# One-hot matrices from 16-bit operands, token column innermost, in a Trainium2 attention-and-experts kernel

## The chip, the cores and the metric

The kernel runs on one core of one Trainium2 chip. The metric is the device time of one execution in microseconds. The profile names the engines: PE is TensorE (matrix products; PEld is its weight load), DVE is VectorE, ACT is ScalarE, POOL is GpSimd and SP is SyncE, which only issues transfers.

## The reference

Three steps follow each other. Lines are left out at "...".

```python
def _attn_ref(q, k, v, g_norm):            # 8 batches, 8 heads, 576 tokens, 64 wide
    kv = np.einsum('bhsd,bhse->bhde', k, v)
    out = np.einsum('bhsd,bhde->bhse', q, kv)
    ...                                    # divided by its rms, times g_norm
def _moe_ref(x, w_gate, w1, w2):           # x: 4608 tokens x 512; 8 experts
    cap = N // E                           # 576 tokens for each expert
    logits = x @ w_gate
    order = np.argsort(-logits.flatten())
    for idx in order:                      # greedy, best score first
        tok, e = (int(idx) // E, int(idx) % E)
        if assigned[tok] >= 0 or counts[e] >= cap:
            continue
        assigned[tok] = e
        counts[e] += 1
    ...
        h = np.maximum(x[mask] @ w1[e], 0.0)
        out[mask] = h @ w2[e]
def _moe2_ref(x, w_in, w_out):             # 512 -> 2048 -> 512
    h = x @ w_in
    return (h * np.cos(h)) @ w_out
```

What matters here is the assignment: it gives each expert a list of exactly 576 tokens, and the kernel needs that list as row numbers, because it gathers those rows of x and later scatters the results with indirect transfers.

## The kernel before, in words

**Stages.** The first 148 us or so hold the attention, which writes the normalised rows of x to a table in device memory (`x_rows`). Then a router of eight *phases* (`Router.phase`, k = 0 to 7) finds, phase by phase, the expert that fills up next and its 576 tokens. Phase 0 runs before the experts' work, phases 1 to 7 are spread between the expert products of the experts before. The rest is 16 units of 288 tokens (two for each expert): products with w1 (`h`), with w2 (`y`), with w_in and the cosine (`h2`), and with w_out (`outs`), all in three-term 16-bit products.

**A phase.** It picks each token's best open expert (`m`, `oh`, `mx`, `ohb`), searches the 576th best score in eight rounds of comparing and counting (`cmp`, `cn`, `g`, `nS`), takes the winning expert (`wi` are the rows of its weights, which POOL then loads), and numbers the chosen tokens: `po` is each token's place in the list, or 0 for a token not chosen. The token numbers are laid out as 128 partitions x 36 columns (`NCOL`).

**The list.** The place p = 32 c + r of each token is taken apart into r = p & 31 (`qi`) and c = p >> 5 (`ci`). For 12 columns at a time (a *group*, three groups in a phase) VectorE forms `A`, 128 x 12 x 32, which is 1 where r equals the position in the last dimension; `Bm` (named `B` in the profile), 128 x 12 x 20, the same for c; and `Bi` (named `Bm` in the profile), 128 x 12 x 2 x 20, which is that times the two halves of the token's number (`C.ids`: number >> 6 and number & 63). TensorE then adds up 36 products `A[column] x Bi[column]`, 32 x 40 each, in one PSUM tile `p`. `low`, `new`, `idx` and `edge` read it and put the row numbers together, and POOL gathers the rows of x by `idx`.

**What sets the order.** The program is recorded by a planner (`Sched`, `Meter`): each instruction is charged a time by its shape, not by its type (`us = 0.07 + 0.06 * scalars + n / 960` for most VectorE operations), and the router's steps are slipped between the expert products where these planned clocks leave room. Each engine then runs its list strictly in that order. A step more, or a longer one, so moves other steps. The tile `pq` in PSUM has one buffer, and the transposes of x and the small products of the weights' scales (`psb`) share it.

**Lines.** `Router.phase` stands at line 274, the place's parts at 423, the groups at 430 to 445, `make_consts` with the counter `i32` and `ids` at 474 to 505. All instructions carry the line of one recording helper (687), so rows are told apart by the names of tiles.

Of the kernel before, what the change touches and what calls it, by code (L numbers as in the profile page):

```python
# [8 lines left out]
F32 = mybir.dt.float32  # L9
F16 = mybir.dt.float16  # L10
BF = mybir.dt.bfloat16
I32 = mybir.dt.int32
AF = mybir.ActivationFunctionType
OP = mybir.AluOpType
# [7 lines left out]
NCOL = 36  # L22
# [236 lines left out]
class Router:  # L259
# [14 lines left out]
    def phase(self, k):  # L274
        nc, wk, C, L = self.nc, self.wk, self.C, self.L
        V = nc.vector
# [6 lines left out]
        else:  # L283
# [23 lines left out]
            base = wk.tile([128, 1], F32, name="base")  # L307
            yield "result"
            nS = None
            for half in range(2):  # L310
                for r in range(4):
# [16 lines left out]
                    p = self.pt()  # L328
# [3 lines left out]
                    else:  # L332
                        for g in range(9):
                            c = slice(4 * g, 4 * g + 4)
# [5 lines left out]
                        p = self.pt()  # L340
# [3 lines left out]
                    g = wk.tile([16, E], BF, name="g1")  # L344
                    V.tensor_scalar(g[0:n], p[0:n, 0:E], CAP - 0.5, step, op0=OP.is_ge, op1=OP.mult)
                    yield "result"
                    p = self.pt()
# [13 lines left out]
            w = wk.tile([128, E], F32, name="w")  # L361
# [25 lines left out]
        if last:  # L387
            eh = None
            w = wk.tile([128, E], F32, name="w")
# [18 lines left out]
        if not last:  # L408
# [9 lines left out]
                               op0=OP.add, op1=OP.mult)  # L418
        po = wk.tile([128, NCOL], F32, name="po")
        V.tensor_add(po, pv[:, 0], pv[:, 1])  # L420
        pi = wk.tile([128, NCOL], I32, name="pi")
        V.tensor_scalar(pi, po, -1.0, None, op0=OP.add)
        qi = wk.tile([128, NCOL], I32, name="qi")
        V.tensor_scalar(qi, pi, 31, None, op0=OP.bitwise_and)
        ci = wk.tile([128, NCOL], I32, name="ci")
        V.tensor_scalar(ci, pi, 5, None, op0=OP.arith_shift_right)
        yield "vector"
        p = self.pt()
        G = 12
        for g in range(NCOL // G):  # L430
            c = slice(g * G, g * G + G)
            A = wk.tile([128, G, 32], BF, name="A", bufs=2)
            V.tensor_tensor(A, qi[:, c, None].to_broadcast([128, G, 32]),
                            C.i32[:, None, :].to_broadcast([128, G, 32]), op=OP.is_equal)
            yield "vector"
            Bm = wk.tile([128, G, 20], BF, name="B1")
            V.tensor_tensor(Bm, ci[:, c, None].to_broadcast([128, G, 20]),
                            C.i32[:, None, 0:20].to_broadcast([128, G, 20]), op=OP.is_equal)
            Bi = wk.tile([128, G, 2, 20], BF, name="Bm", bufs=2)
            V.tensor_tensor(Bi, Bm[:, :, None, :].to_broadcast([128, G, 2, 20]),  # L440
                            C.ids[:, c, :, None].to_broadcast([128, G, 2, 20]), op=OP.mult)
            yield "result"
            for i in range(G):
                nc.tensor.matmul(p[0:32, 0:40], A[:, i, :], Bi[:, i].rearrange("p h s -> p (h s)"), start=(g + i == 0),
                                 stop=(g * G + i == NCOL - 1))
        V.tensor_sub(self.un, self.un, v[:, 0])
        V.tensor_sub(self.un, self.un, v[:, 1])
# [26 lines left out]
def make_consts(nc, sb, w, C):  # L474

    V, G = nc.vector, nc.gpsimd
    jp = w[:, 0:128]
    G.iota(jp, pattern=[[1, 128]], base=0, channel_multiplier=-1)
    C.ident = sb.tile([128, 128], F32, name="ident")
    V.tensor_scalar(C.ident, jp, 0.0, None, op0=OP.is_equal)  # L480
    C.tri = sb.tile([128, 128], BF, name="tri")
    V.tensor_scalar(C.tri, jp, 0.0, None, op0=OP.is_gt)
    C.ones = sb.tile([128, 128], BF, name="ones")
    V.memset(C.ones, 1.0)
    C.i32 = sb.tile([128, 32], F32, name="i32")
    G.iota(C.i32, pattern=[[1, 32]], base=0, channel_multiplier=0, allow_small_or_imprecise_dtypes=True)
    C.i16 = sb.tile([128, 4, 16], F32, name="i16")
    for r in range(4):
        s = 1 << (12 - 4 * r)
        G.iota(C.i16[:, r], pattern=[[s, 16]], base=0, channel_multiplier=0, allow_small_or_imprecise_dtypes=True)  # L490
    i32 = w[0:32, 128:160]
    G.iota(i32, pattern=[[-1, 32]], base=0, channel_multiplier=1)
    C.sel = sb.tile([32, 4, E], F16, name="sel")
    V.tensor_scalar(C.sel.rearrange("p c e -> p (c e)"), i32, 0.0, None, op0=OP.is_equal)
    C.w8 = sb.tile([128, E], F32, name="w8")
    G.iota(C.w8, pattern=[[-1, E]], base=E, channel_multiplier=0, allow_small_or_imprecise_dtypes=True)
    C.ip4 = sb.tile([128, 4], F32, name="ip4")
    G.iota(C.ip4, pattern=[[128, 4]], base=0, channel_multiplier=1, allow_small_or_imprecise_dtypes=True)
    ids = w[:, 160:160 + NCOL]
    G.iota(ids.rearrange("p (s r) -> p s r", r=RB), pattern=[[2 * S, B // 2], [1, RB]], base=0, channel_multiplier=RB)  # L500
    C.ids = sb.tile([128, NCOL, 2], F32, name="ids")
    V.tensor_scalar(w[:, 200:200 + NCOL], ids, 6, None, op0=OP.arith_shift_right)
    V.tensor_copy(C.ids[:, :, 0], w[:, 200:200 + NCOL])
    V.tensor_scalar(w[:, 240:240 + NCOL], ids, 63, None, op0=OP.bitwise_and)
    V.tensor_copy(C.ids[:, :, 1], w[:, 240:240 + NCOL])

# [365 lines left out]
class Moe:  # L874
# [103 lines left out]
    def dense(self, sc):  # L978
# [35 lines left out]
        for i, (which, a, j) in enumerate(units):  # L1014
# [5 lines left out]
            if j == 0:  # L1020
                side = "A" if side == "B" else "B"
                if side in self.used:
# [413 lines left out]
def body(ctx, tc, q, k, v, g_norm, w_gate, w1, w2, w_in, w_out, out):  # L1436
# [4 lines left out]
    sm = ctx.enter_context(tc.tile_pool(name="sm", bufs=2))  # L1441
    C = Consts()
    make_consts(nc, pers, sm.tile([128, 512], I32, name="dG", bufs=DG), C)
    gcol = pers.tile([128, 1], F32, name="gcol")
    for s in range(2):
# [158 lines left out]
```

## Time and profile before

| | us |
|---|---|
| median of 3 runs | 1442.72 |
| lowest and highest | 1441.85, 1450.02 |
| the profiled execution, its own time | 1443.92 |
| span of its trace | 1442.2 |
| PE busy | 1330.7 (92%) |
| DVE busy | 901.0 (62%) |
| ACT busy | 615.4 (43%) |
| POOL busy | 165.3 (11%) |

Busy shares are means over the whole span; what an engine's work is worth is read in its stretch. A matmul's duration holds its way through the engine's pipeline, so that twelve of 0.18 us each may stand in 0.47 us. The chain of waits goes back from the last instruction, at each step to what released it.

### The profile page before, as it was taken

The page shows a single profiled execution, that of the slowest core. Times are in us where ns is not written, and L with a number is a line of the kernel's source. Part 1 is how long each engine was busy: PE and PEld are TensorE (multiplying, and loading weights), DVE is VectorE, ACT ScalarE, POOL GpSimd, SP SyncE. Part 2 cuts the span into 40 slices and gives each one's busy share as a digit, 9 for nine tenths or more (in the row PEclk, how much of TensorE's full clock was granted, in tenths as well). Part 3 has the DMA queues.
Part 4 walks back from the last instruction along what each step waited for, and adds up shares of the span by engine and source line. Part 5 has one row for each costly group of instructions (what it writes and reads, how often), then busy time and mean ns, then how long its engine had stood idle before and what let it go on. Part 6 is the DMA issues. An engine that isn't in the chain of part 4 may idle for free.

```text
span 1442.2 us, 28591 instructions
## 1 busy us (share of the span) xinstructions
PE 1330.7 (92%) x12072; PEld 906.4 (63%) x12072; DVE 901.0 (62%) x2136; ACT 615.4 (43%) x1031; POOL 165.3 (11%) x195
## 2 busy tenths in 40 slices
PE   5777258989999999999999999999999999999997
PEld 4665235746666674757575756767676667667663
DVE  2668888879578674786578656654466336544350
ACT  2567364737255430546054602553356125424140
POOL 0000130012012011040003100320021002000000
PEclk9889569999999999999999999999999999999999
DMA  8896452213023011041003200220022002000000
GB/s 295 306 353 245 156 161 92 74 67 104 8 67 93 16 59 45 1 127 44 8 8 101 66 9 16 95 75 1 15 93 74 8 16 74 16 1 15 8 8 22
DMA packets 40368, 109.63 MB, mean 76 GB/s; under 512 B 4272, under 2 KB 12464, under 8 KB 39728
## 3 DMA queue, kind: packets, MB, share of 16 engines
q0 software_dynamic: 15744, 62.70, 13.0%
q1 hardware_dynamic: 23808, 45.09, 9.0%
q8 instruction: 94, 1.54, 0.4%
q14 instruction: 34, 0.28, 0.1%
q10 hardware_dynamic: 688, 0.02, 0.0%
HBM read 88.78 MB, written 19.02 MB: 75 GB/s over the span
## 4 chain that ended last, share of the span: by engine, by line
PE 83%; DVE 9%; issue 3%; ACT 2%; DMA 2%; POOL 1%; ACTq 0%; POOLq 0%; DVEq 0%
PE ph L687 74%; PE pr L687 3%; PE pT L687 2%; PE P L687 1%; PE pO L687 1%; PE pq L687 1%; DVE stB L687 1%; DVE SS L687 1%; DMA wgr<-in_moe_w_gate_dram 1%; DVE stA L687 1%; DVE cmp L687 1%; DVE eg L687 1%; DVE qTs L687 1%; DVE w1s L687 1%; DVE wout L687 0%
## 5 line engine op out<-in xcount | busy, mean ns | idle before, releaser
L687 PE MATMUL ph<-wout,gT 128*128 128x512 f16 x1728 | 392.4, 381 | 7.3 <-ACT wout L687 3.9
L687 PE MATMUL ph<-yT,win 128*128 128x288 f16 x3072 | 384.1, 286 | 1.4 <-DVE eg L687 1.4
L687 PEld LDWEIGHTS <-win 128*128 128x128 f16 x3072 | 297.9, 98 | 81.3 <-DVE eg L687 2.4
L687 PEld LDWEIGHTS <-gT 128*128 128x128 f16 x1728 | 162.4, 98 | 193.7 <-issue 7.2
L687 ACT ACTIVATE ek<-ph,quarter,us 128x576 int32<-128x576 f32 x128 | 106.1, 829 | 324.3 <-PE ph L687 308.8
L687 PE MATMUL ph<-xT,w1s 128*128 128x288 f16 x1536 | 201.3, 290 | 7.5 <-DVE hT L687 6.5
L687 PE MATMUL ph<-hT,w2s 128*128 128x288 f16 x1536 | 201.7, 286 | 0.0
L687 DVE SCALAR_TENSOR_TENSOR et<-ph,us,ek 128x576 f32<-128x576 f32 x128 | 104.6, 817 | 132.4 <-ACT ek L687 129.6
L687 PEld LDWEIGHTS <-w1s 128*128 128x128 f16 x1536 | 148.8, 99 | 47.7 <-issue 4.9
L687 PEld LDWEIGHTS <-w2s 128*128 128x128 f16 x1536 | 146.4, 98 | 36.2
L687 POOL DMA_INDIRECT out_dram<-eg,idx x36 | 38.3, 1064 | 620.5 <-DVE scT L687 291.5
L687 DVE SCALAR_TENSOR_TENSOR eg<-ph,cG,et 128x576 f32<-128x576 f32 x128 | 103.6, 809 | 2.7 <-ACT et L687 1.3
L687 DVE TENSOR_TENSOR gT<-eg,gT 128x576 f16<-128x576 f32 (+2 forms) x192 | 99.6, 550 | 0.7
L687 ACT ACTIVATE et<-et,qtr 128x576 f32<-128x576 f32 x128 | 97.8, 764 | 0.0
L687 ACT ACTIVATE gT<-eg 128x576 f16<-128x576 f32 (+2 forms) x192 | 92.0, 511 | 12.0 <-DVE eg L687 12.0
L687 DVE TENSOR_TENSOR eg<-ph,scT 128x512 f32<-128x512 f32 x36 | 24.9, 692 | 104.5 <-PE ph L687 100.7
L687 ACT ACTIVATE yT<-ph,sy 128x576 f16<-128x576 f32 x32 | 21.9, 736 | 139.9 <-DVE sy L687 137.4
L687 DVE SCALAR_TENSOR_TENSOR hT<-ph,hT 128x576 f16<-128x576 f32 x64 | 48.2, 755 | 49.4 <-ACT hT L687 49.2
L687 ACT ACTIVATE hT<-ph 128x576 f16<-128x576 f32 x64 | 41.1, 645 | 88.7 <-PE ph L687 87.2
L687 POOL DMA_INDIRECT io<-x_rows,idx x35 | 39.7, 1135 | 254.4 <-PE pq L687 202.4
L687 POOL DMA_INDIRECT stA<-in_moe_w_dram,wi x28 | 35.5, 1270 | 199.8 <-issue 193.1
L687 PE MATMUL pO<-KV,qTs 64*64 64x72 f32 x1152 | 38.2, 248 | 13.2 <-issue 12.3
(213 smaller groups left out, 1299.2 us busy)
## 6 DMA issues: line engine op xcount, KB each, us to landing
kt<-in_k_dram SPq DMA_DIRECT2D x16, 576.0 KB, 6.2
vt<-in_v_dram SPq DMA_DIRECT2D x16, 576.0 KB, 7.6
qt<-in_q_dram SPq DMA_DIRECT2D x16, 576.0 KB, 7.8
io<-in_moe_w_in_dram SPq DMA_DIRECT2D x16, 512.0 KB, 6.9
io<-in_moe_w_out_dram SPq DMA_DIRECT2D x16, 512.0 KB, 3.6
x_rows<-xs POOLq DMA_DIRECT2D x3, 2340.0 KB
x_rows<-wout POOLq DMA_DIRECT2D x1, 2340.0 KB
out_dram<-eg,idx POOLq DMA_INDIRECT x36
```

The lines of the kernel that those rows point to most:

```text
L687: return f(*a, **kw)
```

## The change

The one-hot matrices are laid out with the 12 token columns as the last dimension and formed from bfloat16 operands alone. Both parts of the place go into one tile `qc`, which one more instruction (`CAST qb<-qc`, 128 x 72) turns to bfloat16. The counter is written out for all 12 columns (`i32g`, 128 x 32 x 12, one CAST at the program's start), and `ids` is kept as two rows of 36 in bfloat16. TensorE reads `A[:, :, i]` and `Bi[:, :, :, i]`: the elements of one product lie 12 elements (24 bytes) apart where they lay side by side. The numbers and shapes of the products, and of the three VectorE operations in a group, are as before.

```diff
@@ Router.phase
-        qi = wk.tile([128, NCOL], I32, name="qi")
-        V.tensor_scalar(qi, pi, 31, None, op0=OP.bitwise_and)
-        ci = wk.tile([128, NCOL], I32, name="ci")
-        V.tensor_scalar(ci, pi, 5, None, op0=OP.arith_shift_right)
+        qc = wk.tile([128, 2, NCOL], I32, name="qc")
+        V.tensor_scalar(qc[:, 0], pi, 31, None, op0=OP.bitwise_and)
+        V.tensor_scalar(qc[:, 1], pi, 5, None, op0=OP.arith_shift_right)
+        qb = wk.tile([128, 2, NCOL], BF, name="qb")
+        V.tensor_copy(qb, qc)
...
-            A = wk.tile([128, G, 32], BF, name="A", bufs=2)
-            V.tensor_tensor(A, qi[:, c, None].to_broadcast([128, G, 32]),
-                            C.i32[:, None, :].to_broadcast([128, G, 32]), op=OP.is_equal)
+            A = wk.tile([128, 32, G], BF, name="A", bufs=2)
+            V.tensor_tensor(A, qb[:, 0, None, c].to_broadcast([128, 32, G]), C.i32g, op=OP.is_equal)
...
-            Bm = wk.tile([128, G, 20], BF, name="B1")
-            V.tensor_tensor(Bm, ci[:, c, None].to_broadcast([128, G, 20]),
-                            C.i32[:, None, 0:20].to_broadcast([128, G, 20]), op=OP.is_equal)
-            Bi = wk.tile([128, G, 2, 20], BF, name="Bm", bufs=2)
-            V.tensor_tensor(Bi, Bm[:, :, None, :].to_broadcast([128, G, 2, 20]),
-                            C.ids[:, c, :, None].to_broadcast([128, G, 2, 20]), op=OP.mult)
+            Bm = wk.tile([128, 20, G], BF, name="B1")
+            V.tensor_tensor(Bm, qb[:, 1, None, c].to_broadcast([128, 20, G]), C.i32g[:, 0:20], op=OP.is_equal)
+            Bi = wk.tile([128, 2, 20, G], BF, name="Bm", bufs=2)
+            V.tensor_tensor(Bi, Bm[:, None].to_broadcast([128, 2, 20, G]),
+                            C.ids[:, :, None, c].to_broadcast([128, 2, 20, G]), op=OP.mult)
...
-                nc.tensor.matmul(p[0:32, 0:40], A[:, i, :], Bi[:, i].rearrange("p h s -> p (h s)"), start=(g + i == 0),
+                nc.tensor.matmul(p[0:32, 0:40], A[:, :, i], Bi[:, :, :, i].rearrange("p h s -> p (h s)"), start=(g + i == 0),
@@ make_consts
-    C.i32 = sb.tile([128, 32], F32, name="i32")
-    G.iota(C.i32, pattern=[[1, 32]], base=0, channel_multiplier=0, allow_small_or_imprecise_dtypes=True)
+    C.i32g = sb.tile([128, 32, 12], BF, name="i32g")
+    i32 = w[:, 280:312]
+    G.iota(i32, pattern=[[1, 32]], base=0, channel_multiplier=0)
+    V.tensor_copy(C.i32g, i32[:, :, None].to_broadcast([128, 32, 12]))
...
-    C.ids = sb.tile([128, NCOL, 2], F32, name="ids")
+    C.ids = sb.tile([128, 2, NCOL], BF, name="ids")
...
-    V.tensor_copy(C.ids[:, :, 0], w[:, 200:200 + NCOL])
+    V.tensor_copy(C.ids[:, 0], w[:, 200:200 + NCOL])
...
-    V.tensor_copy(C.ids[:, :, 1], w[:, 240:240 + NCOL])
+    V.tensor_copy(C.ids[:, 1], w[:, 240:240 + NCOL])
```

The planner charges the new CAST, and some steps move. Outside phase 0 and the stretch between phases 1 and 2 only a few rows do.

VectorE in phase 1, from the place to the next search; before (`psm`, `psb`: the weights' scale of the next expert; `low` to `idx`: the list; `m`: the next phase's start):

```order
L687 TENSOR_SCALAR qi<-pi 128x36
L687 TENSOR_SCALAR ci<-pi 128x36
...
L687 TENSOR_TENSOR un<-un,v 128x36 x2
L687 COPY low<-pr 32x20
L687 SCALAR_TENSOR_TENSOR new<-pr,low 32x1 x4
L687 TENSOR_TENSOR idx<-edge,new 128x1
L687 SCALAR_TENSOR_TENSOR idx<-pr,low 32x4 x4
L687 TENSOR_REDUCE psm<-am_4506 128x1
L687 TENSOR_SCALAR psb<-psm,g_95 128x1
L687 TENSOR_REDUCE m<-L 128x36
```

and after:

```order
L688 TENSOR_SCALAR qc<-pi 128x36 x2
L688 CAST qb<-qc 128x72
...
L688 TENSOR_TENSOR un<-un,v 128x36 x2
L688 TENSOR_REDUCE psm<-am_4509 128x1
L688 TENSOR_SCALAR psb<-psm,g_96 128x1
L688 TENSOR_SCALAR peb<-pq 128x1
L688 TENSOR_SCALAR s_4535<-peb 128x1
L688 TENSOR_TENSOR sg<-s_4535,gcol 128x1
L688 COPY low<-pr 32x20
L688 SCALAR_TENSOR_TENSOR new<-pr,low 32x1 x4
L688 TENSOR_TENSOR idx<-edge,new 128x1
```

The scale of the next expert's w1 now stands ahead of the list. On TensorE its product `pq<-psb,ones` follows 3 products with w_out behind phase 1's last group where it followed 12, and 18 instead of 15 products with w_out stand ahead of the first group.

ScalarE in phase 0 (`sti`: the first expert's w1 as loaded; `win<-stB`: a piece of w_in split); before:

```order
L687 ACTIVATE junk,am<-stB 128x1024 x2
L687 ACTIVATE win_102<-stB,s_105 128x2x512 x2
L687 ACTIVATE junk,am_2489<-sti 128x1024 x4
L687 ACTIVATE w1s_2455<-sti,sg 128x1024 x3
```

and after:

```order
L688 ACTIVATE junk,am<-stB 128x1024 x2
L688 ACTIVATE junk,am_2490<-sti 128x1024 x4
L688 ACTIVATE win_103<-stB,s_106 128x2x512 x2
L688 ACTIVATE w1s_2456<-sti,sg 128x1024 x3
```

The two splits of w_in now stand behind the four sums over w1 and directly ahead of the first split of w1. VectorE's and TensorE's lists in phase 0 are the same but for the new names and the CAST.

## Rows read from the trace of the kernel before

**Rows 1.** the page: the span, and each engine's busy us (share) x instructions

```profile
span 1442.2 us, 28591 instructions
PE 1330.7 (92%) x12072; PEld 906.4 (63%) x12072; DVE 901.0 (62%) x2136; ACT 615.4 (43%) x1031; POOL 165.3 (11%) x195
```

**Rows 2.** stretches: length, busy us by PE, PEld, DVE, ACT, POOL; PEclk, DMA share

```profile
178.00:183.00 5.00, 1.12 (x24) 1.18 (x25) 4.83 (x13) 2.14 (x3) 3.15 (x3) 0.50 0.83 238
215.00:391.00 176.00, 159.85 (x1257) 106.88 (x1255) 143.90 (x334) 91.21 (x139) 17.85 (x19) 0.96 0.23 72
600.00:960.00 360.00, 358.51 (x2741) 237.90 (x2740) 241.03 (x593) 148.97 (x232) 61.37 (x62) 1.00 0.17 55
```

**Rows 3.** groups by line and form: busy us, mean ns, idle before

```profile
L687 DVE TENSOR_TENSOR A<-qi,i 128x384 bf16<-128x384 int32 x24 | 13.3, 553 | 0.0
L687 DVE TENSOR_TENSOR B<-ci,i 128x240 bf16<-128x240 int32 x24 | 9.6, 401 | 0.0
L687 DVE TENSOR_TENSOR Bm<-B,ids 128x480 bf16<-128x480 bf16 x24 | 15.8, 658 | 0.8
L687 DVE SCALAR_TENSOR_TENSOR stA<-dG,stA 128x512 int32<-128x512 int32 x16 | 11.0, 687 | 0.3
L687 DVE TENSOR_SCALAR stA<-dG 128x512 int32<-128x512 int32 x16 | 6.7, 419 | 0.0
L687 DVE TENSOR_REDUCE SS<-sq 128x8 f32<-128x512 f32 x32 | 21.6, 676 | 0.0
L687 DVE TENSOR_REDUCE L<-LR 128x72 f32<-128x576 f32 x4 | 4.8, 1209 | 0.1
```

**Rows 4.** timeline of phase 0: start us, us, engine, form, count [idle before <-releaser]

```profile
176.80 2.19 ACT L687 ACTIVATE win<-stB,s 128x1024 f16<-128x1024 f32 x2 [4.92 <-DVE s L687]
178.16 0.18 DVE L687 TENSOR_SCALAR pi<-po 128x36 int32<-128x36 f32 x1
178.38 0.18 DVE L687 TENSOR_SCALAR qi<-pi 128x36 int32<-128x36 int32 x1
...
178.60 0.56 DVE L687 TENSOR_TENSOR A<-qi,i 128x384 bf16<-128x384 int32 x1
...
184.90 0.95 POOL L687 DMA_INDIRECT et<-x_rows,idx  x1 [3.14 <-DVE idx L687]
...
189.70 0.69 DVE L687 TENSOR_TENSOR et<-et 128x512 f32<-128x512 f32 x1
```

**Rows 5.** chain that ended last, same stretch: start us, us, what

```profile
180.59 5.84 DMA sti<-in_moe_w_dram,wi
...
187.48 0.20 ACT junk L687
...
188.10 1.19 DVE win L687
...
189.78 1.23 ACT w1s L687
```

**Rows 6.** chain that ended last, phase 1 and the phase's next search

```profile
317.42 0.40 PE pr L687 x12
317.82 2.70 PE ph L687 x12
...
336.70 0.36 PE pr L687 x9
```

**Rows 7.** TensorE's waits from 391 us on, longest first: us, times, longest

```profile
PE ph L687 <- DVE eg L687: 2.6, 2, 1.9
PE pq L687 <- DVE psb L687: 1.3, 1, 1.3
PE pr L687 <- DVE cmp L687: 0.3, 1, 0.3
PE pq L687 <- DVE xT L687: 0.2, 1, 0.2
```

**Rows 8.** TensorE's waits from 216 to 391 us, that on a shared PSUM tile

```profile
PE pq L687 <- DVE xT L687: 1.4, 1, 1.4
```

## The prediction

> **What bounds the kernel now.** I read the page first, for the span of 1442.2 us and TensorE's share of it, 92% [rows 1]. A mean says little, so the stretches came next. From 600 to 960 us TensorE is busy 358.51 of 360.00 us and VectorE 241.03: time there is saved or lost only by TensorE. [...] Third came the groups by form, for the price of the three operations that change: 553, 401 and 658 ns, 24 of each [rows 3]. Last the chain of waits at the eight places: in phase 0 it does not go through these operations but through the load of the first expert's w1 [rows 5]; in phase 1 it is TensorE throughout, and the twelve products of a group stand in it with 0.40 us [rows 6]. From 391 us on no wait of TensorE ends on `A` or `Bm` at all [rows 7].
>
> So the operations that get cheaper are covered, and the products that read them are not, in 21 of the 24 groups.
>
> **VectorE's operations.** `A` and `B` differ by 144 elements and 152 ns, 1.06 ns an element; `Bm` lies on the same line (553 + 96 x 1.06 = 655, measured 658), though it has a 16-bit operand already [rows 3]. The trace has no two-operand operation with 16-bit operands alone. Bounds from the nearest rows: nothing saved, or what a one-operand instruction on 512 elements shows against a two-operand one, 419 against 687 ns, so 0.52 ns less an element [rows 3]. With 384 + 240 + 480 = 1104 elements the upper bound is 0.57 us a group, 1.7 us a phase, 13.8 us in all. Against it stands the added CAST. It depends on the second part of the place, and a dependent step starts 0.22 us after the one before (178.16, 178.38) [rows 4]: 0.2 us a phase, 1.8 us in all. I take the upper bound, the row nearest to two elements a step: VectorE works 12 us less.
>
> [...]
>
> **What of that is on the path.** *Phase 0:* the list is ready 1.7 - 0.2 = 1.5 us earlier, and POOL's gather, at 184.90, with it [rows 4]. But w1 lands at 180.59 + 5.84 = 186.43, its sums end at 187.68, and VectorE reaches the first gathered tile only at 189.70, since w1's scale stands ahead of it on that engine [rows 4, 5]. Nothing gained; late next is w1's load, as now. *Phases 1 to 7:* TensorE covers them [rows 6, 7]; if that cover were gone, each phase would be worth 1.5 us. I count 0, with 1.5 us (phase 0) as the nearer end and 12 us (all phases) as the far one.
>
> **The moved steps.** In phase 0 the two splits of w_in (2.19 us, at 176.80 before) now follow the last sum over w1 [rows 4]. From 187.68 they end at 189.87; w1's split began at 189.78 [rows 5]: +0.1 us, and up to +2.2 if they started late. In phase 1 `psb` moves ahead of the list. Its product comes three products behind the last group, each some 2.70 / 12 = 0.23 us [rows 6], 0.7 us of cover, and the 18 products ahead of the first group give 0.7 us more than before. The list then waits for five small steps on VectorE; POOL's gather and the transposes of x behind it come some 2 us later, and the order puts those transposes 24 products later too. The one wait on the shared tile there, 1.4 us [rows 8], has the same form in the new order (transposes, then `psb`): I leave it. Between no such wait and two, this is -1.4 to +1.4; I take 0. At the start, the CAST of the counter has `A`'s size (0.55 us) [rows 3] and lies before the first keys and values are needed: 0.
>
> **TensorE's products.** Their number and shapes stay, but both operands are read 24 bytes apart. No product in the trace reads 16-bit columns so; zero is the lower bound. The nearest rows of a strided read are VectorE's: a reduction that steps 32 bytes takes 1209 ns for 576 elements, while one over adjacent elements takes 676 for 512 and so 744 for 576 [rows 3]. With a fixed part of 744 - 576 x 1.06 = 133 ns, a strided element costs 1.87 ns, 1.76 times the adjacent one, 0.81 ns more. If TensorE pays those 0.81 ns for each of 40 moving and 32 weight columns, a product gets 58 ns dearer: the upper bound. I take the factor, not the nanoseconds, because TensorE's own price of a column is in the trace: nine products of 60 columns hold the chain for 0.36 us, 40 ns each, twelve of 40 columns for 0.40 us, 33 ns each [rows 6], so 0.33 ns a column. A factor of 1.76 makes 40 columns cost what 70 do: +10 ns, with the weight load still covered by the product before it. On 21 groups, 252 products: **+2.5 us**; the bounds are 0 and 252 x 58 ns = 14.6 us. Phase 0's 36 products stand where TensorE waits for VectorE, so they cost nothing.
>
> [...]
>
> **The sum.** 0 (phase 0) + 0.1 (splits) + 0 (moved steps) + 2.5 (strided products) = +2.6 us. The profiled execution took 1443.92, so 1446.5 in its terms. It lies 1.2 us above the median of the runs shown, 1442.72; measured against that, as the result will be, **1445.3 us**.
>
> **The rivals.**
> - *The stride is free.* The weight load and the product hide it, as one hides the other now. Then +0.1, with the moved steps 1441.4 to 1444.2. For it: 33 ns for 40 columns is more than 40 x 0.33 = 13 ns, so there is slack in each product.
> - *The saving reaches the path.* An earlier list lets POOL gather earlier, and the loads queued behind it on POOL too. It decides if the gathered rows, and not w1, were what phase 0 waited for: 1.5 us less, 1441.2; with each phase's part, 12 us less, 1430.7. Against it: the chain at 180.59 is w1's transfer [rows 5].
> - *The stride is dear.* Each product waits by the nanoseconds of VectorE's row, in its weight load and in its columns, right on TensorE's path: up to +14.6, so 1450 to 1457.4. It decides from 57 ns a product, where 1% (14.4 us) is reached. This is the one that ends slower.
> - *The operations don't get cheaper.* The pair of operands, one of them repeated, may still go one element at a time. Phase 0's list would be 0.2 us later, under the same cover: the time of the forecast, with VectorE's rows unchanged at about 550, 400 and 660 ns.
>
> **Chances.** The forecast (5 to 20 ns a product and the moved steps) 0.50; free stride 0.18; saving on the path 0.12; dear stride 0.14; no cheaper operations 0.06. The range leaves out the far part of the third case and the upper half of the fourth, about 0.15 together: **1440 to 1453**. A measurement of this kernel can tell about 1% from no change. All of VectorE's saving on the path is 0.8%, so faster by over 1% needs something that I haven't seen: 0.03. Slower by over 1% is the end of the fourth case and a stall that the new order brings: 0.07. Within 1%: 0.90.
>
> **What would show it.** In the new profile `A`, `B` and `Bm` near 350, 275 and 405 ns, and VectorE's busy time about 12 us lower: that step is right. The twelve products of a group near 0.50 us in the chain, where 0.40 stood, show the stride's price; 0.40 makes it free, 1.0 makes it dear. In phase 0 the chain should still go through w1's transfer, with the gather near 183.4 us. The prediction is wrong if TensorE gets a new wait on `psb`, `low` or `xT` between 320 and 400 us of more than 1.5 us, or if the first products with w1 start over 1 us earlier or later.

## The result and the profile after

The changed kernel takes **1457.27 us** (median of six runs, 1455.45 to 1461.72); the kernel before took 1442.26 in the six runs beside them. The ratio is 1.0094, with a 95% interval of 1.0074 to 1.0115: 13.6 us by the ratio, 15.0 by the two medians. 1445.3 was forecast, with a range to 1453: the time lies outside, on the side of the rival "the stride is dear". The profiled execution took 1459.92 us, 16.0 more than that of before.

The page of the changed kernel (busy us, share, instructions), against [rows 1]:

```profile
span 1458.2 us, 28602 instructions
PE 1348.6 (92%) x12072; PEld 919.2 (63%) x12072; DVE 889.8 (61%) x2145; ACT 615.6 (42%) x1031; POOL 163.4 (11%) x195
```

VectorE works 11.2 us less, as the change means it to. TensorE works 17.9 us more, with exactly as many products as before. So the next view is the groups by form (busy us, mean ns | idle before). First VectorE, against [rows 3]:

```profile
L688 DVE TENSOR_TENSOR A<-qb,i32g 128x384 bf16<-128x384 bf16 x24 | 8.5, 354 | 4.6 <-PE pr L688 4.4
L688 DVE TENSOR_TENSOR B<-qb,i32g 128x240 bf16<-128x240 bf16 x24 | 6.6, 277 | 0.0
L688 DVE TENSOR_TENSOR Bm<-B,ids 128x480 bf16<-128x480 bf16 x24 | 9.8, 408 | 0.8
L688 DVE CAST qb<-qc 128x72 bf16<-128x72 int32 x8 | 1.9, 237 | 0.3
...
L688 PE MATMUL pr<-Bm,A 128*32 128x40 bf16 x288 | 25.9, 255 | 3.5 <-DVE Bm L688 3.5
```

The operations fell from 553, 401 and 658 ns to 354, 277 and 408. The last row is the products that read them; before, it was:

```profile
L687 PE MATMUL pr<-Bm,A 128*32 128x40 bf16 x288 | 11.5, 183 | 5.4 <-DVE Bm L687 5.4
```

That is (25.9 - 11.5) / 288 = 50 ns more for each. The other 3.5 us of TensorE's 17.9 are no more than single executions differ by: in the kernels below whose products take 11.5 or 11.6 us, TensorE is busy between 1330.4 and 1343.4 us. `A` now has idle time before it that ends on `pr`: VectorE waits for TensorE to give one of `A`'s two buffers back. TensorE's own wait for `Bm` fell, from 5.4 to 3.5 us, so no cover or buffer is missing on VectorE's side. What the dearer products cost is read where TensorE is the path, in the chain of waits in phase 1 (start us, us, what), against [rows 6]:

```profile
315.18 3.89 PE ph L688 x18
319.07 1.02 PE pr L688 x12
320.09 2.70 PE ph L688 x12
322.78 1.02 PE pr L688 x12
```

A group of twelve stands in it with 1.02 us where it had 0.40, 52 ns more for each product. The twelve expert products between two groups take 2.70 us as before. In 21 groups that is 21 x 0.62 = 13.0 us. How much of it reaches the end is seen from the first and last products with w_in, one row for the whole run (shortest, median and longest ns, then first and last start), before and after:

```profile
L687 PE MATMUL ph<-yT,win x3072: 282/286/297, 254.4 to 1399.3; 128*128 128x288 f16 x192
L688 PE MATMUL ph<-yT,win x3072: 282/286/298, 255.4 to 1413.6; 128*128 128x288 f16 x192
```

So 1.0 us of the 16.0 is there before the first of them, 13.3 arises between them, and the last 1.7 comes after them. That middle stretch leaves out the start-up, and I use it again below, always as its length against the 1144.9 us of before. How far it repeats is seen from two runs below that are the kernel before with products added at its very end: there the products with w_in start at 254.7 and 250.2 us, and the stretch is 1145.1 and 1145.3 us long. So 1.0 us ahead of the first start means nothing.

The last 1.7 us are a matter of the clock. The first 3.5 us of the products with w_out behind TensorE's last wait, before and after (length, busy us of PE, PEld, DVE, ACT and POOL, granted clock, DMA share):

```profile
1403.80:1407.30 3.50, 3.50 (x17) 1.60 (x18) 2.00 (x6) 0.58 (x1) 0.00 (x0) 1.00 0.02 5
1418.00:1421.50 3.50, 3.50 (x9) 1.26 (x10) 2.05 (x6) 0.63 (x1) 0.00 (x0) 0.51 0.02 5
```

In both kernels TensorE has just waited 1.86 and 0.77 us for VectorE. In the changed kernel's execution the clock then stands at 0.50, and TensorE does 8 products fewer. The traces of the kernels below have the same end: from the last start of a product with w_in it takes 42.9 us without this fall and 44.2 to 44.6 with it, and both cases occur with strided as well as with adjacent products.

Two stretches, against [rows 2] (length, busy us of PE, PEld, DVE, ACT and POOL, granted clock, DMA share):

```profile
215.00:391.00 176.00, 158.83 (x1225) 106.92 (x1224) 140.46 (x328) 91.00 (x139) 17.09 (x19) 0.96 0.22 72
600.00:960.00 360.00, 359.80 (x2716) 241.61 (x2715) 236.29 (x600) 147.94 (x230) 54.48 (x55) 1.00 0.15 48
```

In both stretches the clock is granted as before. From 600 to 960 us TensorE did 2716 products where it had done 2741, still without a pause: it is not waiting, its work got longer. TensorE's waits from 391 us on say the same (us, times, longest), against [rows 7]:

```profile
PE ph L688 <- DVE eg L688: 2.6, 2, 1.9
PE pq L688 <- DVE psb L688: 1.4, 1, 1.4
PE pr L688 <- DVE cmp L688: 0.3, 1, 0.3
PE pq L688 <- DVE xT L688: 0.2, 1, 0.2
```

From 216 to 391 us the wait on `xT` is 1.4 us as before [rows 8]; one of 0.9 us on `cmp`, at 308.86 us, is new. Phase 1's first group starts only 0.65 us later against the first product with w_in than before, which is the length of the 3 products with w_out that now stand ahead of it.

Last the timeline of phase 0, against [rows 4] (start us, us, engine, operation, count, idle before and its releaser):

```profile
179.15 0.23 DVE L688 TENSOR_SCALAR pi<-po 128x36 int32<-128x36 f32 x1
...
179.96 0.36 DVE L688 TENSOR_TENSOR A<-qb,i32g 128x384 bf16<-128x384 bf16 x1
...
182.10 0.36 DVE L688 TENSOR_TENSOR A<-qb,i32g 128x384 bf16<-128x384 bf16 x1 [0.24 <-PE pr L688]
...
183.15 1.06 PE L688 MATMUL pr<-Bm,A 128*32 128x40 bf16 x12 [0.18 <-DVE Bm L688]
...
184.45 0.66 DVE L688 SCALAR_TENSOR_TENSOR idx<-pr,low 32x5 int32<-32x5 f32 x4
...
187.27 0.16 DVE L688 TENSOR_REDUCE psm<-am 128x1 f32<-128x4 f32 x1 [1.50 <-ACT junk L688]
...
189.27 0.69 DVE L688 TENSOR_TENSOR et<-et 128x512 f32<-128x512 f32 x1
```

Before, `idx` came at:

```profile
183.97 0.66 DVE L687 SCALAR_TENSOR_TENSOR idx<-pr,low 32x5 int32<-32x5 f32 x4
```

From `pi` to `idx` it is 5.30 us, against 5.81 before: 0.5 us earlier, not the 1.5 I expected. From `pi` to `A` it takes 0.81 us where it took 0.44, the third `A` waits for a buffer, and a group takes 1.06 us here too. None of it matters: VectorE then stands idle for 1.50 us until ScalarE has summed w1, and `et` comes only after that. The first products with w1 start at 196.4 us, against 196.9. The chain of the changed kernel goes back no further than 208.17 us, so it does not show whether phase 0 still hangs on w1's transfer.

### The profile page after: what moved, and what is told of

Read it like the earlier page. It is cut to its first block, busy times and chain, and to the rows that moved or that the text cites. A ratio compares the mean times of both kernels' runs of the same rounds, so it can differ in the third digit from the quotient of the medians.

```text
span 1458.2 us, 28602 instructions
## 1 busy us (share of the span) xinstructions
PE 1348.6 (92%) x12072; PEld 919.2 (63%) x12072; DVE 889.8 (61%) x2145; ACT 615.6 (42%) x1031; POOL 163.4 (11%) x195
## 4 chain that ended last, share of the span: by engine, by line
PE 77%; DVE 5%; issue 2%; ACT 1%; POOL 0%; DMA 0%; POOLq 0%; ACTq 0%; DVEq 0%
PE ph L688 72%; PE pr L688 3%; PE pq L688 1%; DVE eg L688 1%; DVE wout L688 1%; DMA stB<-in_moe_w_dram,wi 0%; DVE stB L688 0%; DVE cmp L688 0%; ACT ek L688 0%; DVE yT L688 0%; DVE et L688 0%; DVE stA L688 0%; DVE gT L688 0%; DVE xT L688 0%; POOL out_dram L688 0%
## 5 line engine op out<-in xcount | busy, mean ns | idle before, releaser
L688 ACT ACTIVATE gT<-eg 128x576 f16<-128x576 f32 (+2 forms) x192 | 92.0, 511 | 11.5 <-DVE eg L688 11.5
L688 DVE TENSOR_TENSOR eg<-ph,scT 128x512 f32<-128x512 f32 x36 | 24.9, 692 | 104.8 <-PE ph L688 100.9
```

What stands on the lines that cost most here:

```text
L688: return f(*a, **kw)
```

## The experiments

The theory after the result: all of the loss is the stride of TensorE's reads, paid in TensorE's own time; VectorE's saving and the moved steps are worth nothing. The rivals: the new order of steps costs it (the planner charges the added CASTs); a missing cover or buffer on VectorE costs it; TensorE's two operands each add a part, so that one could stay strided.

**VectorE writes what TensorE reads side by side.** The shortest way back to adjacent reads: the operands of VectorE's operations stay as in the changed kernel, only the result is written permuted. In the first kernel for both matrices, then for `A` alone and for `Bi` alone:

```diff
-            A = wk.tile([128, 32, G], BF, name="A", bufs=2)
-            V.tensor_tensor(A, qb[...], C.i32g, op=OP.is_equal)
+            A = wk.tile([128, G, 32], BF, name="A", bufs=2)
+            V.tensor_tensor(A.rearrange("p g r -> p r g"), qb[...], C.i32g, op=OP.is_equal)
-            Bi = wk.tile([128, 2, 20, G], BF, name="Bm", bufs=2)
-            V.tensor_tensor(Bi, Bm[...], C.ids[...], op=OP.mult)
+            Bi = wk.tile([128, G, 2, 20], BF, name="Bm", bufs=2)
+            V.tensor_tensor(Bi.rearrange("p g h s -> p h s g"), Bm[...], C.ids[...], op=OP.mult)
...
-   matmul(..., A[:, :, i], Bi[:, :, :, i].rearrange("p h s -> p (h s)"), ...)
+   matmul(..., A[:, i, :], Bi[:, i].rearrange("p h s -> p (h s)"), ...)
```

Both:

> The changed kernel with its operands, its order of instructions and its loops, but VectorE writes A and Bi so that the 32 weight columns and the 40 moving columns of a product lie side by side again. Theory (the stride is dear): a group of 12 products goes from 1.02 us in the chain of the changed kernel back to 0.40 us; 21 groups under TensorE's path give back 13.0 us, so 1442 to 1446 us. Rival (the moved steps cost): the order is the changed one, so the time stays at 1453 or above. A and Bi are written with a step and should lose their gain: 550 and 660 ns or more each, which both theories count at nothing.

`A` alone:

> The changed kernel with only the weights (A) side by side; the 40 moving columns stay 24 bytes apart. If each strided element costs a fixed time and weights and columns add up (72 elements in 85 ns, 1.1 ns each), a product takes 40 x 1.1 + 32 x 0.33 = 55 ns, a group 0.65 us, the kernel 1447 to 1450 us. If the moving columns alone carry the price, 85 ns and 1455 us or more. If the weights alone carry it, 33 ns, 0.40 us a group, 1442 to 1445 us.

`Bi` alone:

> The changed kernel with only the moving columns (Bi) side by side; the 32 weight columns stay 24 bytes apart. If weights and columns add up: 32 x 1.1 + 40 x 0.33 = 48 ns a product, 0.58 us a group, 1446 to 1449 us. If the moving columns alone carry the price: 0.40 us a group, 1442 to 1445 us. If the weights alone: 1.02 us, 1455 us or more.

Measured against 1446.09 of the kernel before: both 1495.74, ratio 1.0341 (1.0322 to 1.0360); `A` alone 1458.61, 1.0087 (1.0066 to 1.0109); `Bi` alone 1466.74, 1.0145 (1.0124 to 1.0166). The groups of the kernel with both:

```profile
L689 DVE TENSOR_TENSOR Bm<-B,ids 128x480 bf16<-128x480 bf16 x24 | 53.3, 2221 | 0.8
L689 DVE TENSOR_TENSOR A<-qb,i32g 128x384 bf16<-128x384 bf16 x24 | 46.2, 1925 | 0.2
...
L689 PE MATMUL pr<-Bm,A 128*32 128x40 bf16 x288 | 11.5, 184 | 46.6 <-DVE Bm L689 32.6 <-DVE un L689 8.6 <-DVE psm L689 2.7
```

The products are back at 11.5 us, with the changed kernel's operands and its added CAST: the stride is what made them dear. But the times tell nothing about the rest, because the edit brought a cost of its own of which my expectations had only a small part (550 and 660 ns or more): writing 16-bit elements 64 or 80 bytes apart takes VectorE more than five times as long as writing them side by side (1925 against 354 ns, 2221 against 408). TensorE's cover, which hides the 4.8 us that before spends on these operations in a phase (three times 553 + 401 + 658 ns), does not hide three times 1925 + 2221 ns, 12.4 us: TensorE waits 32.6 us for `Bm`.

The halves are confounded by the same writes. The products' busy time is still readable. It is 24.9 us with only the columns of `Bi` strided and 19.9 with only the weights of `A` strided; 25.9 is for both. So the two prices do not add up; the dearer one nearly is the whole.

**The products by themselves.** At the end of the kernel before, sets of 24 products of 32 weights x 40 columns, with the step between elements as the only difference, in the weights, in the columns, or in both:

```diff
+    p, x = M.ph(), M.win[0]
+    for step in (1, 2, 4, 6, 8, 12, 16, 32):
+        for wst, cst in ((step, step),) if step == 1 else ((step, 1), (1, step), (step, step)):
+            nc.tensor.matmul(p[:, 1, 0:128], x[:, 2, 0:128], x[:, 3, 0:128], start=True, stop=True)
+            for i in range(24):
+                nc.tensor.matmul(p[0:32, 0, 0:40], x[:, i % 2, 0:32 * wst].rearrange("p (r t) -> p r t", t=wst)[:, :, 0],
+                                 x[:, 2 + i % 2, 0:40 * cst].rearrange("p (r t) -> p r t", t=cst)[:, :, 0],
+                                 start=True, stop=True)
```

> The kernel before with 22 sets of 24 products of 32 x 40 added behind its last product, their results unused: weights, moving columns or both read with a step of 1, 2, 4, 6, 8, 12, 16 and 32 elements of 2 bytes; a product of 128 columns stands between the sets. If the price is one of stride in bytes beyond some size, sets with a small step take 33 ns a product as adjacent ones do, and the sets from some step on 55 (one operand) to 85 ns (both), the same for 12, 16 and 32. If each step costs by its length, the time goes on rising to 32. Rival (the stride is not the cause): all 22 sets take 26 to 35 ns a product.

One run took 1473.57 us, 27.5 more than without the sets. Its rows show that the price depends on the length of the step, and that a step of 4 bytes costs nothing (29.2 ns a product, as adjacent). From about 1444.5 us on, within the sets at 12 bytes, the granted clock fell to 0.50, after the expert products had ended. So the larger steps were measured again at a clock of 1.00, with 24 products of 512 columns ahead of each set; the second version (one run, 1558.53 us) had no step of 32 bytes and ten VectorE operations of 384 16-bit elements added:

```diff
-            nc.tensor.matmul(p[:, 1, 0:128], x[:, 2, 0:128], x[:, 3, 0:128], start=True, stop=True)
+            for i in range(24):
+                nc.tensor.matmul(p[:, 1], x[:, i % 2, 0:128], x[:, 3, 0:512], start=True, stop=True)
...
+    for step in (1, 2, 4, 8, 16):      # first a strided write, then strided reads
+        V.tensor_tensor(w[step], x0, x1, op=OP.mult)
+        V.tensor_tensor(o, r[step], r[step], op=OP.mult)
```

> The separate sets again, each between 24 products of 512 columns, so that TensorE's granted clock is 1.00 where the first sets ran partly at 0.50. If the price of a strided element is a time and not a number of TensorE's cycles, the sets at 24 and 64 bytes keep 74 to 80 ns for columns and 62 to 66 ns for weights; if it is cycles, they fall to about half. Behind them ten operations of VectorE on 384 16-bit elements: the result written, or the operands read, with a step of 1, 2, 4, 8 and 16 elements. The operations that wrote with a step of 64 and 80 bytes took 1925 and 2221 ns; if any step costs that, all from 2 on are near 1.9 us; if the loss is only that of pairs, near 0.55 us at small steps.

Stretches of the second version, each just one set (length, TensorE's busy us, products with the neighbours that reach in, clock, DMA). In order: adjacent; 8 bytes in the weights, in the columns, in both; 24 bytes in the weights, in the columns, in both:

```profile
1434.99:1435.70 0.71, 0.71 (x26) 1.00 0.78 317
...
1458.93:1459.85 0.92, 0.92 (x26) 1.00 0.00 0
1465.12:1466.15 1.03, 1.03 (x26) 1.00 0.00 0
1471.42:1472.49 1.07, 1.07 (x26) 1.00 0.00 0
...
1518.89:1520.40 1.51, 1.51 (x26) 1.00 0.00 0
1525.67:1527.53 1.86, 1.86 (x26) 1.00 0.00 0
1532.81:1534.77 1.96, 1.96 (x26) 1.00 0.04 8
```

A length divided by 24 is taken as the price of a product. It holds the change to the next set, 3.5 to 4.7 ns of each price: between the starts of a set's own products it is 25.7 ns adjacent, and 58.7, 72.4 and 77.0 at 24 bytes. The last set (64 bytes, both) has no product behind it; its 73.6 is between starts and stands lower by that much. All steps, in ns a product, from the second version (32 bytes: from the first, at a clock of 0.50):

| step, bytes | weights strided | columns strided | both |
|---|---|---|---|
| 2 (adjacent) | | | 29.2 |
| 4 | 29.2 | 29.3 | 29.2 |
| 8 | 37.8 | 42.5 | 44.2 |
| 12 | 51.2 | 59.8 | 61.3 |
| 16 | 64.5 | 77.0 | 78.9 |
| 24 | 62.3 | 77.1 | 81.5 |
| 32 | 66.7 | 78.4 | 80.7 |
| 64 | 61.1 | 73.7 | 73.6 |

In the first version, the same set of 24 bytes in the columns, at the lower clock:

```profile
1454.82:1456.67 1.85, 1.85 (x25) 0.50 0.00 0
```

1.85 / 24 = 77 ns at a clock of 0.50, 77.1 at 1.00. The other sets from 16 bytes on that stand in both versions agree within 1.4 ns too. So from there on it is a time, not a number of TensorE's steps; at 8 bytes the lower clock was not measured. For an element it is 77.1 / 40 = 1.93 ns in the columns and 62.3 / 32 = 1.95 in the weights at 24 bytes (1.81 and 1.83 between starts), hardly other than at 16 or 64, and 1.06 to 1.18 at 8 bytes. It stops growing at 16 bytes.

**The same columns in blocks of two and of four.** If a step of 4 bytes is free, both sides can have what they want: two token columns side by side, so that VectorE's last dimension holds two, and the elements that TensorE reads lie 4 bytes apart. In blocks of four they lie 8 bytes apart. Everything else, the order of the steps too, is as in the changed kernel. With J = 2 or 4 and K = 12 / J:

```diff
-            A = wk.tile([128, 32, G], BF, name="A", bufs=2)
-            V.tensor_tensor(A, qb[:, 0, None, c].to_broadcast([128, 32, G]), C.i32g, op=OP.is_equal)
+            A = wk.tile([128, K, 32, J], BF, name="A", bufs=2)
+            qv = qb[:, :, c].rearrange("p t (b j) -> p t b j", j=J)
+            V.tensor_tensor(A, qv[:, 0, :, None].to_broadcast([128, K, 32, J]),
+                            C.i32g[:, None, :, 0:J].to_broadcast([128, K, 32, J]), op=OP.is_equal)
...
-   matmul(..., A[:, :, i], Bi[:, :, :, i].rearrange("p h s -> p (h s)"), ...)
+   matmul(..., A[:, i // J, :, i % J], Bi[:, :, i // J, :, i % J], ...)
```

Blocks of two:

> The changed kernel, in the same order, with columns in blocks of two: A is 128 x 6 x 32 x 2 and Bi 128 x 2 x 6 x 20 x 2, so the elements of a product lie 4 bytes apart where they lay 24 apart, and the last dimension of VectorE's operations has two elements. Theory (the stride is dear, and a step of 4 bytes is free, 29.2 ns as in the adjacent set): a group of products at 0.40 us in the chain again, 13.0 us less than the changed kernel, so 1442 to 1445 us; VectorE's saving (rows of A, B, Bm near 350, 275, 405 ns if pairs still go two at a time) is hidden and gives nothing. Rival 1 (VectorE's saving is worth something once the products don't eat it): 1.5 us a phase, down to 12 us below the kernel before, 1431 to 1439. Rival 2 (the moved steps cost too): 1447 or more.

Blocks of four:

> As the blocks of two, but of four: the elements of a product lie 8 bytes apart. The separate sets gave 43.8 ns for 8 bytes in both operands, 14.6 ns over the adjacent set. If that price adds on the path: 252 x 14.6 ns = 3.7 us over the blocks of two, a group near 0.57 us in the chain. [...]

Measured against 1444.88 (35 runs): blocks of two 1444.19, ratio 1.0000 (0.9984 to 1.0016); blocks of four 1449.51, 1.0026 (1.0008 to 1.0043). The groups with blocks of two:

```profile
L693 DVE TENSOR_TENSOR A<-qb,i32g 128x384 bf16<-128x384 bf16 x24 | 12.0, 500 | 1.1 <-PE pr L693 0.8
L693 DVE TENSOR_TENSOR Bm<-B,ids 128x480 bf16<-128x480 bf16 x24 | 9.8, 408 | 0.8
L693 DVE TENSOR_TENSOR B<-qb,i32g 128x240 bf16<-128x240 bf16 x24 | 8.9, 369 | 0.0
...
L693 PE MATMUL pr<-Bm,A 128*32 128x40 bf16 x288 | 11.5, 183 | 5.0 <-DVE Bm L693 5.0
```

A group in the chain, with blocks of two:

```profile
318.51 0.40 PE pr L693 x12
```

and with blocks of four:

```profile
317.86 0.57 PE pr L693 x12
```

`A` and `B` take 500 and 369 ns here, not the 350 and 275 expected. With 4 bytes the whole loss is gone, in the changed kernel's own order of steps. With 8 bytes a product costs 14 ns more, 21 x 0.17 = 3.6 us; the stretch between the first and last product with w_in is 0.4 us longer than before with blocks of two and 4.4 with blocks of four.

**The order of the steps and VectorE's saving, each by itself.** The first kernel has the 16-bit operands and the changed kernel's order, but the old layout, in which the place's element (for `Bi` the token number's) is repeated along the last dimension. For `A`:

```diff
-            V.tensor_tensor(A, qb[:, 0, None, c].to_broadcast([128, 32, G]), C.i32g, op=OP.is_equal)
+            V.tensor_tensor(A, qb[:, 0, c, None].to_broadcast([128, G, 32]), C.i32g, op=OP.is_equal)
...
-   matmul(..., A[:, :, i], Bi[:, :, :, i].rearrange("p h s -> p (h s)"), ...)
+   matmul(..., A[:, i, :], Bi[:, i].rearrange("p h s -> p (h s)"), ...)
```

> The changed kernel, in the same order, with the old layouts and loops (A 128 x 12 x 32, Bi 128 x 12 x 2 x 20, row position last) on the 16-bit operands: products read adjacent elements and VectorE writes adjacent ones. One operand then repeats one element along the last dimension. If VectorE takes pairs whenever all is 16 bits: A, B, Bm near 350, 275, 405 ns. If the repeated element keeps it at one at a time: 550, 400, 660. Either way the products are at 0.40 us a group. Theory (all of the loss is the stride): 1442 to 1445 us. Rival (the moved steps cost): 1447 or more.

The second is that with blocks of two, with the two CASTs not charged by the planner, so that the steps keep the order of before into phase 2:

```diff
-        V.tensor_copy(qb, qc)
+        nc.nc.vector.tensor_copy(qb, qc)
```

> The blocks of two, with the two new CASTs left out of the planner's clocks, so that the order up to phase 2 is that of the kernel before (later a few rows differ). Against the blocks of two it shows what the moved steps between phases 0 and 2 are worth: theory 0, within 2 us of the blocks of two; rival, over 2 us.

Measured against the same 1444.88: 1444.27 each, ratios 0.9993 (0.9976 to 1.0010) and 0.9996 (0.9980 to 1.0012). The first one's groups:

```profile
L688 DVE TENSOR_TENSOR Bm<-B,ids 128x480 bf16<-128x480 bf16 x24 | 15.8, 658 | 0.8
L688 DVE TENSOR_TENSOR A<-qb,i32g 128x384 bf16<-128x384 bf16 x24 | 13.3, 555 | 0.2
```

Three kernels with adjacent or nearly adjacent reads, and no difference among them: with the new order and dear operations (VectorE busy 903.0 us), with the new order and cheaper ones (895.8), with the old order and cheaper ones (895.2). So the moved steps cost nothing and VectorE's saving gains nothing, both within some 0.2%. A single trace is coarser than these medians: the first kernel's profiled execution was its slowest, 1451.77 us, and its stretch between the products with w_in is 3.6 us longer than before, though its groups stand in the chain with 0.40 us. In part that is a fall of the clock to 0.50 for 3.4 us at 965.8 us, behind a wait for `psb` of 2.0 us where before has 1.3. The rows also show what the layout was for: 16-bit operands alone change nothing (555 against 553 ns) while one operand repeats a single element along the last dimension.

**One operand strided, without the dear writes.** Blocks of two for `A` only, so that the columns stay 24 bytes apart, and for `Bi` only, so that the weights do; the edits are the halves of the one above.

Weights near, columns 24 bytes apart:

> The changed kernel, same order, with the weights (A) in blocks of two columns, 4 bytes apart, and the 40 moving columns still 24 bytes apart; VectorE writes adjacent elements everywhere. The separate sets gave 77 ns for strided columns alone and 80 for both, 29 adjacent. If the dearer of the two sets the time (weight load and product overlap): a group about 0.98 us in the chain, 0.04 us less than with both strided, and the kernel 12 us above the blocks of two, 1455 to 1458 us. If the two prices added up, half would go: 1449 to 1451.

Columns near, weights 24 bytes apart:

> The other half: moving columns in blocks of two, 4 bytes apart, weights still 24 bytes apart. Dearer of the two: a product at the 63 to 65 ns of the separate sets for strided weights, a group 0.78 us, so 252 x 34 ns = 8.6 us above the blocks of two, 1451 to 1455 us. Adding up: 1449 to 1451. Weights free: 1444.

Measured against 1445.42: with strided columns 1461.86, ratio 1.0108 (1.0074 to 1.0141), with strided weights 1454.56, 1.0060 (1.0038 to 1.0082). The first lies 4 us above the range expected; of its trace's difference from before, 5.3 us stand ahead of the first product with w_in, where one and the same program differs by 4.5. A group in the chain with strided columns:

```profile
323.36 0.97 PE pr L690 x12
```

and with strided weights:

```profile
320.14 0.80 PE pr L692 x12
```

0.97 and 0.80 us by themselves, 1.02 together: the two prices overlap, and the dearer side sets nearly all of it. In the changed kernel's trace the weight loads stand beside the products: from 319.00 us a group's twelve loads take 0.90 us, its twelve products 1.09 us. By 21 groups it is 12.0 and 8.4 us; the stretch between the products with w_in got 12.4 and 10.0 us longer, 0.6 and 0.8 of it by one more wait on `eg`. Making one operand near is not enough. No kernel tried here is faster than the kernel before.

## Why the prediction was wrong, step by step

- **What bounds the kernel: right.** TensorE is the path in 21 of 24 groups, VectorE's operations are covered and the products are not. The result is this sentence: VectorE 11.2 us less, TensorE's products 14.4 us more, the end 15 us later.
- **VectorE's operations: right.** 354, 277 and 408 ns, where 350, 275 and 405 were expected; VectorE's busy time fell 11.2 us, where 12 were. The upper bound was the right choice, and the fourth rival (no cheaper operations) is out. No row had shown its "two elements a step" then; in the changed kernel an element costs (354 - 277) / 144 = 0.53 ns, half of the 1.06 of before.
- **Nothing of that on the path: right**, by the kernel with blocks of two, which keeps about half of the saving (VectorE busy 895.8 us, where the same steps take 903.0 with dear operations and 889.8 in the changed kernel) and is no faster. The early list of phase 0 came 0.5 us instead of 1.5 us earlier; the added steps up to `A` cost 0.37 us instead of 0.2, and the products cost time there as well, so "they cost nothing" holds only because w1's sums hide the list.
- **w_in's splits, +0.1 us: right.** From the last sum over w1 to its split it is 2.12 us, against 2.10.
- **The moved steps, 0: right.** With them 1.0000 and without them 0.9996. No new wait on `psb`, `low` or `xT` is in the rows.
- **The strided products, +2.5 us: wrong, and the whole miss.** The mechanism and the count stand: 252 products on TensorE's path. The term measures 13.0 us in the chain, 52 ns a product where I took 10. The step that failed is "I take the factor, not the nanoseconds". I had VectorE's price of a strided element, 1.87 ns [rows 3], and turned it into a factor on TensorE's price of an adjacent column, 0.33 ns. The price measured for TensorE is 1.93 ns an element, alike at both clocks: here the nanoseconds carried over, and the factor did not. That the read itself takes the time on either engine fits this and is not shown. Forty columns by 1.87 ns are 75 ns in place of the 33 in the chain, so +42 ns and 10.6 us, which would have given 1453.4. The 33 ns hold the change to the next products, which the stride leaves as it is; in place of the 26.5 ns between the starts in a group it is +48 ns and 12.2 us.
- **The rival "the stride is dear": this is what happened**, at 52 of its 58 ns. Its bound was near for a wrong reason: it added weights and columns and kept the adjacent price below them, and the two errors nearly cancel, which is luck. What holds is nearly the larger of the two, in place of the adjacent price. At 0.14, with its upper half left out of the range, it had too little: the one strided read in the trace spoke for it, and against it stood only that TensorE is another engine.

The chain gives 13.0 us and the medians 15.0 (interval 10.7 to 16.6, from the ratio). In the traces 13.3 us lie between the products with w_in; of the other 2.7, 1.0 lie ahead of them, where the same program differs by 4.5 us from run to run (250.2 to 254.7 us), and 1.7 behind them, in the stretch at a clock of 0.50. So the products' 13.0 us are all of the difference between the two traces that the change itself is shown to make.

## What to carry to other kernels

Before a layout is turned round for the engine that writes it, price the reads of the engine that is the path: 24 bytes between 16-bit elements went with VectorE operations 31 to 38% cheaper and made TensorE's products 2.5 times as dear (1.02 against 0.40 us a group). From 16 bytes on, VectorE's price of a strided element in nanoseconds was a good estimate of TensorE's (1.87 against 1.84 to 2.08), and a factor on the adjacent price was not; at 4 bytes the two engines differ (next section). Of weights and columns take the larger (at 24 bytes 62.3 and 77.1 ns a product alone, 81.5 in both). Where both engines have a claim, blocks of two 16-bit elements were free for TensorE (0.40 us a group, as before) and kept part of VectorE's gain (500, 369 and 408 ns); that can pay only where VectorE is the path, which no kernel here shows.

## What the runs showed of the hardware that I had not expected

- TensorE reads 16-bit elements 4 bytes apart at no price (29.2 ns a product, as adjacent), 8 bytes apart at 1.06 to 1.18 ns an element, and from 16 bytes on at 1.84 to 2.08, in weights and columns alike. From 16 bytes on the price is the same at a clock of 0.50 and of 1.00, within 1.4 ns a product.
- VectorE's reads at 16 bytes have nearly the same price an element; its strided writes are far dearer. In the second version with sets, operations of 384 elements, each in a stretch of its own (length, VectorE's busy us, count): adjacent; read 4 bytes apart; written 8 bytes apart; read 8 bytes apart; written 16 bytes apart; read 16 bytes apart (both operands read the same row):

```profile
1433.01:1433.35 0.34, 0.34 (x1) 1.00 0.08 24
...
1434.43:1434.97 0.54, 0.54 (x1) 1.00 0.13 53
1435.02:1436.03 1.01, 1.01 (x1) 1.00 0.52 211
1436.07:1436.62 0.55, 0.55 (x1) 1.00 0.00 0
1436.67:1438.53 1.86, 1.86 (x1) 1.00 0.00 0
1438.57:1439.42 0.85, 0.85 (x1) 1.00 0.00 0
```

With the 133 ns that the prediction estimated as an operation's fixed part, a read at 16 bytes is (850 - 133) / 384 = 1.87 ns an element, the price of the reduction in [rows 3] and nearly TensorE's; a write at 16 bytes is 4.5. Read 4 or 8 bytes apart, an operation takes 0.54 and 0.55 us against 0.34 adjacent: VectorE pays at 4 bytes, where TensorE does not, and no more at 8.
- With a last dimension of two elements VectorE keeps part of its saving in `A` (500 ns, against 553 before and 354 in the changed kernel) and all of it in `Bm` (408, against 658 and 408). The short dimension need not be what `A` loses by: its counter is read in pairs that lie 24 bytes apart, and no operand of `Bm` is. With the counter read in fours, in the kernel with blocks of four, `A` takes 356 ns. No run separates the two.
